# Attention and bilinear MoE on one core: seven products of halves in batch 1 too, and two units of w moved from stage 2 into stage 1

## The chip, the cores and the metric

The kernel runs on one core of a Trainium2 chip. The metric is the device time of one execution in microseconds (us), lower being better; the output must agree with the reference in shape, type and value.

A core has a matrix engine (TensorE, PE in the profile), a vector engine (VectorE, DVE), a scalar engine (ScalarE, ACT), GpSimd (POOL, unused here) and SyncE (SP), which in this kernel only issues transfers (DMAs). Matmuls write into PSUM, from which VectorE and ScalarE read.

## The reference

Eight batches of 512 tokens with 8 heads of 64, and 32 state rows for each batch and head. Attention in both directions gives 512 + 32 rows of 512 for each batch, and a bilinear expert turns each row into 512 outputs:

```python
scores = scale * x @ state.T;  a = softmax(scores);   xread = a @ state
scores2 = scale * state @ x.T; a2 = softmax(scores2); sread = a2 @ x
rows = concatenate([xread, sread], axis=2)          # heads merged: 4608 rows of 512
h = ((rows @ w1) * (rows @ w2)) @ w3                # 512 -> 1024 -> 1024
out = h @ w_out                                     # 1024 -> 512
```

The kernel folds w3 and w_out into one matrix of 1024 x 512 (`wo`), and the state of a batch with w1 and w2 into `sw`, so that (a @ state) @ w1 becomes a @ (state @ w1). All large products are made of three float32r matmuls (hi x lo, hi x hi, lo x hi), for which each operand is split: `split` is a ScalarE cast to `hi` (L97) and a VectorE subtract to `lo` (L98).

## The kernel before, in words

The program has a prologue (weights are converted, batch 0's attention and stage 1 run), then batches 0 to 7 in turn, then the 256 state rows (`state_rows`). A batch has these parts:

- **Stage 1** (`stage1_sums`, L301): eight tiles `ft` of 128 columns of the 1024; each takes 12 matmuls of 128x512 (L310) into a two-bank PSUM tile (`two_banks`, pool `ps_2`, three tiles in rotation). ScalarE copies one bank out (L394, or L291 in a plain batch), VectorE multiplies it with the other.
- **Stage 2, plain** (`stage2`, L328): four tiles `tt` of 128 tokens, 24 matmuls of 128x512 each (L324). Batches 0 and 1 have it.
- **Stage 2 by quarters** (`stage2_quarters`, L434): seven products of half-size operands (a Strassen-like scheme: a11, s3, a12, a22, s2, s1, s4), 24 matmuls of 128x256 each (`product`, L428). Batches 2 to 7 have it (`fast_batch`, L490). It needs sums and differences of halves of the hidden values, made in `hidden_quarters` (L389) and during stage 2, and of halves of `wo`, made once by `combine_weights(k)` for k = 0 to 3 (two sums L371, four differences L377, one split into `t_hi` and `t_lo`). Before, k = 0 and 1 are made in batch 1's stage 1, after ft 3 and ft 7, and k = 2 and 3 in its stage 2.
- **Attention of the next batch**, hidden among the above: `scores` (8 matmuls L147 on each half of the rows, then maxima and exponentials), its softmax sums (from L210), `at` (transpose L221 and split), a transpose and 16 block moves by SyncE (L228, L171), and `read_state` of the present batch (`reads[b]`, 64 small matmuls L243, L248, L252, 16 moves).
- **w of the next batch** (`sw_steps`, L264): four units w[0] to w[3]. A unit is a two-bank PSUM tile filled by 16 matmuls of 64x32 weights (L147), and a split of 128x1024 from it, whose cast and subtract both read PSUM. Stage 1's ft 0 to 3 use w[0] and w[1], ft 4 to 7 use w[2] and w[3].

In `fast_batch` reads[b] and scores stand after ft 3; `stage2_quarters` runs w[0], w[1] and the softmax after its first product (a11), and w[2] and w[3] after the second (s3).

TensorE and SyncE run in the order in which the code is written (`manual_schedule`). ScalarE's and VectorE's order is set by a scheduler when the program is built, with priority for the lines under `tc.high_priority()`; on the chip each engine runs its list in order, and waits where a semaphore tells it to. A PSUM tile is written again only when all readers of what it held are done. `x_d`, `x_s` and `e2` have one buffer each, `st` two; their loads are issued after ft 3 (`load_tokens`, `load_x`), those of batches 1 and 2 before that at the end of batch 0's stage 2.

Of the kernel before, what the change touches and what calls it, by code (L numbers as in the profile page):

```python
# [29 lines left out]
P = 128  # L30
# [3 lines left out]
LAST = 5  # L34
PARTS = {0: (640, 1024), 1: (512, 1024)}
WARM = 15
PLAIN = 2

@with_exitstack
def attn_bilinear_kernel(  # L40
# [302 lines left out]
    def side_steps(b):


        if b == B:
            return [[reads[b - 1]], [], [], []]
        scores, reads[b], a2 = attention_steps(b)
        w = sw_steps(b)
        softmax = scores()  # L350
        first = partial(islice, softmax, 3)
        if b == 1:
            def rest():

                with tc.issue_after(stored[0].ins):
                    yield from softmax

            return [[first], [reads[0], w[0], w[1]], [], [rest], [w[2], w[3]], []]

        product = partial(islice, softmax, 1)  # L360
        loads = [partial(load_tokens, b), partial(load_x, b + 1)]
        return [[w[0], w[1], product, reads[b - 1], *loads, w[2], w[3], lambda: softmax], [], [], []]
# [23 lines left out]
    def by_two(t):  # L386
        return t.rearrange("p (k n) -> p k n", k=2)

    def hidden_quarters(ps, ft, q):  # L389
        a_sb = tmp_tile()  # L390
        p, kk = divmod(ft, 2)
        first, second = slice(0, HT), slice(HT, S)
        with tc.high_priority():
            nc.scalar.copy(out=a_sb, in_=ps[:, 0])  # L394
            if ft < QF:
                if kk == 0:
                    q["raw"].append(main.tile([P, 2, NF], F32, name="g_x", bufs=2))
                nc.vector.tensor_tensor(out=q["raw"][p][:, kk], in0=a_sb, in1=ps[:, 1], op=ALU.mult)  # L398
            else:
                if ft == QF:  # L400
                    q["r22"] = late.tile([P, QF, HT], F32, name="r22")
                nc.vector.tensor_tensor(out=a_sb[:, first], in0=a_sb[:, first], in1=ps[:, 1, first], op=ALU.mult)  # L402
                nc.vector.tensor_tensor(out=q["r22"][:, ft - QF], in0=a_sb[:, second], in1=ps[:, 1, second], op=ALU.mult)
        if ft == 0:
            q["a11"], q["s3"] = quarter_pairs(), quarter_pairs()
        elif ft == QF:
            q["a12"] = quarter_pairs()
        if ft >= QF:
            split(*(t[:, kk] for t in q["a12"][p - 2]), a_sb[:, first])
            if kk:  # L410
                i = p - 2
                raw, r22 = q["raw"][i], q["r22"][:, 2 * i:2 * i + 2]
                nc.vector.tensor_tensor(out=raw[:, :, second], in0=raw[:, :, second], in1=r22, op=ALU.add)
                nc.vector.tensor_tensor(out=raw[:, :, first], in0=raw[:, :, second], in1=raw[:, :, first], op=ALU.subtract)
        elif kk:
# [3 lines left out]
            nc.vector.tensor_tensor(out=s3, in0=raw[:, :, first], in1=raw[:, :, second], op=ALU.subtract)
            split(*q["s3"][p], s3)  # L420
# [11 lines left out]
                    )  # L432

    def stage2_quarters(b, q, units):  # L434
        half = lambda o: slice(o * HO, (o + 1) * HO)
        b_part = lambda i, o: (lambda part, k: wo[part][:, i * QF + k, half(o)])
        t_part = lambda j: (lambda part, k: t_parts[part][:, j, k])
        sum2 = lambda out, x, y: nc.vector.tensor_tensor(out=out, in0=x, in1=y, op=ALU.add)  # L438
        c11, c21, m7, m1 = (tmp_tile() for _ in range(4))

        def stored_quarter(o, rows, cols):
            for tt in range(2):
                first = (2 * rows + tt) * P
# [12 lines left out]
        run(units[3:])
# [58 lines left out]
    def batch_stage2(b, gs):  # L515
        side = side_steps(b + 1)
        for tt in range(NT):
            stage2(gs, tt, [(out[b, tt * P:(tt + 1) * P], 0, P)])
            run(side[tt])
            if tt in (1, 2):  # L520
                combine_weights(tt + 1)


    with tc.tile_pool(name="pro", bufs=2) as pro:
# [108 lines left out]
        for tt in range(NT):
            dests = [(out[0, tt * P:(tt + 1) * P], 0, P)]
            if tt in early:
                store(acc[tt], dests)
            else:
                stage2(gs, tt, dests)
            run(side[tt])
        load_tokens(1)  # L640
        load_x(2)
    late = ctx.enter_context(tc.tile_pool(name="late", bufs=1))
    t_parts = {part: late.tile([P, 4, QF, HO], F32R, name=f"t_{part}") for part in ("hi", "lo")}


    def state_rows():
        n = B * NS
# [4 lines left out]
        for ft in range(FT):  # L652
            quarter, c = divmod(ft * P, NQ)
            ps = two_banks()
            for i in range(2):
# [7 lines left out]
            gs.append([g[:, :n] for g in new_g(ft)])  # L663
# [4 lines left out]
            nc.vector.tensor_tensor(out=sums[:, 0], in0=sums[:, 0], in1=sums[:, 1], op=ALU.mult)  # L668
            split(*gs[-1], sums[:, 0])
# [59 lines left out]
```

## Time and profile before

| | |
|---|---|
| time, median of 3 runs | 496.94 us (496.57 to 497.07) |
| the profiled execution | 496.68 us, span 494.9 us, granted TensorE clock 0.999 |
| batches 1, 2 (first stage 1 matmul to the next batch's) | 49.44, 49.43 us |
| batches 3 to 6 | 48.80 us each |

The span runs from the first to the last instruction in the profile. "PE busy" counts matmuls; "PEld" is the loading of weights, which overlaps. In the timeline a row is: start, busy time, engine, line, operation, out<-in, shapes, count; what stands in brackets is the idle time ahead of the row and what ended it. Matmuls are pipelined, so a row's busy time is longer than the distance to the next row's start, and the distances are what counts.

### The profile page before, as it was taken

The page shows a single profiled execution, that of the slowest core. Times are in us where ns is not written, and L with a number is a line of the kernel's source. Part 1 is how long each engine was busy: PE and PEld are TensorE (multiplying, and loading weights), DVE is VectorE, ACT ScalarE, POOL GpSimd, SP SyncE. Part 2 cuts the span into 40 slices and gives each one's busy share as a digit, 9 for nine tenths or more (in the row PEclk, how much of TensorE's full clock was granted, in tenths as well). Part 3 has the DMA queues.
Part 4 walks back from the last instruction along what each step waited for, and adds up shares of the span by engine and source line. Part 5 has one row for each costly group of instructions (what it writes and reads, how often), then busy time and mean ns, then how long its engine had stood idle before and what let it go on. Part 6 is the DMA issues. An engine that isn't in the chain of part 4 may idle for free.

```text
span 494.9 us, 8790 instructions
## 1 busy us (share of the span) xinstructions
PE 486.4 (98%) x3486; PEld 376.0 (76%) x3486; DVE 375.3 (76%) x584; ACT 238.8 (48%) x371; POOL 0.2 (0%) x4
## 2 busy tenths in 40 slices
PE   8999999999999999999999999999999999999996
PEld 5444467777876868897789778977897888899885
DVE  5669896772679889956995799479948994687770
ACT  4767784443544346613651365137513751453650
POOL 0000000000000000000000000000000000000000
PEclk9999999999999999999999999999999999999999
DMA  8996971013500721430233033303330222001101
GB/s 340 363 386 228 366 280 31 13 47 77 187 8 19 235 50 41 160 110 3 88 114 108 2 110 99 101 3 107 112 90 2 91 52 78 4 3 46 42 1 42
DMA packets 55785, 52.48 MB, mean 106 GB/s; under 512 B 42688, under 2 KB 49856, under 8 KB 51136
## 3 DMA queue, kind: packets, MB, share of 16 engines
q1 hardware_dynamic: 47488, 43.27, 26.6%
q10 hardware_dynamic: 8256, 8.65, 5.0%
q8 instruction: 27, 0.44, 0.4%
q14 instruction: 14, 0.11, 0.1%
HBM read 38.27 MB, written 8.91 MB: 95 GB/s over the span
## 4 chain that ended last, share of the span: by engine, by line
PE 83%; DVE 9%; DMA 3%; ACT 2%; issue 1%; SPq 1%; ACTq 0%; DVEq 0%
PE ps L310 29%; PE ps_o L428 20%; PE ps_o L324 8%; PE ps L147 6%; PE ps_o L555 6%; PE ps L661 3%; PE ps L428 3%; PE ps_o L542 3%; PE ps L542 3%; DMA e<-work 2%; PE ps L662 2%; DVE work L187 1%; DVE m L204 1%; DVE m L190 1%; SPq L171 1%
## 5 line engine op out<-in xcount | busy, mean ns | idle before, releaser
L310 PE MATMUL ps<-at_lo,sw_hi 128*128 128x512 f32 x256 | 101.2, 395 | 0.8 <-ACT g_hi L97 0.8
L310 PE MATMUL ps<-at_hi,sw_hi 128*128 128x512 f32 x256 | 99.7, 390 | 0.0
L310 PE MATMUL ps<-at_hi,sw_lo 128*128 128x512 f32 x256 | 99.6, 389 | 0.0
L394 ACT COPY tmp<-ps 128x512 f32<-128x512 f32 x48 | 28.1, 588 | 89.1 <-PE ps L310 54.4
L310 PEld LDWEIGHTS ps<-at_lo,sw_hi 128*128 128x128 f32 x256 | 48.1, 188 | 17.3 <-DVE g_x L398 3.4
L310 PEld LDWEIGHTS ps<-at_hi,sw_lo 128*128 128x128 f32 x256 | 48.1, 188 | 10.1
L310 PEld LDWEIGHTS ps<-at_hi,sw_hi 128*128 128x128 f32 x256 | 48.1, 188 | 9.6 <-issue 0.2
L97 ACT CAST g_hi<-g_x 128x512 fp32r<-128x512 f32 x48 | 29.2, 621 | 39.5 <-DVE g_x L467 20.4
L398 DVE TENSOR_TENSOR g_x<-tmp,ps 128x512 f32<-128x512 f32 x24 | 16.4, 687 | 36.2 <-ACT tmp L394 36.2
L97 ACT CAST g_hi<-tmp 128x256 fp32r<-128x256 f32 (+1 forms) x54 | 27.1, 503 | 32.4 <-DVE tmp L402 16.8
L98 DVE TENSOR_TENSOR sw_lo<-ps,sw_hi 128x1024 fp32r<-128x1024 f32 (+1 forms) x34 | 38.3, 1149 | 5.2 <-ACT sw_hi L97 5.2
L98 DVE TENSOR_TENSOR g_lo<-g_x,g_hi 128x512 fp32r<-128x512 f32 x48 | 31.6, 682 | 3.1 <-ACT g_hi L97 2.8
L98 DVE TENSOR_TENSOR g_lo<-tmp,g_hi 128x256 fp32r<-128x256 f32 (+1 forms) x54 | 28.8, 535 | 6.2 <-ACT g_hi L97 5.6
L97 ACT CAST sw_hi<-ps 128x1024 fp32r<-128x1024 f32 (+1 forms) x34 | 31.3, 967 | 4.2 <-PE ps L147 4.1
L147 PE MATMUL ps<-w_sb,st 64*32 64x512 f32 (+1 forms) x544 | 31.4, 570 | 0.0
L428 PE MATMUL ps_o<-wo_lo,g_hi 128*128 128x256 f32 x144 | 29.6, 287 | 0.5 <-DVE tmp L438 0.5
L428 PE MATMUL ps_o<-t_lo,g_hi 128*128 128x256 f32 x144 | 29.5, 287 | 0.0
L428 PE MATMUL ps_o<-t_hi,g_hi 128*128 128x256 f32 x144 | 29.0, 283 | 0.0
L428 PE MATMUL ps_o<-wo_hi,g_hi 128*128 128x256 f32 x144 | 29.0, 283 | 0.0
L428 PE MATMUL ps_o<-wo_hi,g_lo 128*128 128x256 f32 x144 | 29.0, 283 | 0.0
L428 PE MATMUL ps_o<-t_hi,g_lo 128*128 128x256 f32 x144 | 29.0, 283 | 0.0
L555 PE MATMUL ps_o<-w_sb,w 128*128 128x512 f32 x64 | 28.5, 599 | 0.0
(113 smaller groups left out, 912.6 us busy)
## 6 DMA issues: line engine op xcount, KB each, us to landing
raw<-in_w_k_dram SPq DMA_DIRECT2D x8, 1024.0 KB, 6.8
x_d<-in_x_d_dram SPq DMA_DIRECT2D x8, 1024.0 KB, 7.0
raw<-in_w_dram SPq DMA_DIRECT2D x8, 1024.0 KB, 6.4
x_s<-in_x_s_dram SPq DMA_DIRECT2D x8, 1024.0 KB, 5.3
out_dram<-tmp ACTq DMA_DIRECT2D x48, 128.0 KB, 2.0
raw<-in_w3t_dram SPq DMA_DIRECT2D x4, 1024.0 KB, 7.5
e<-work SPq DMA_DIRECT2D x96, 32.0 KB, 2.0
sread<-turned SPq DMA_DIRECT2D x128, 4.0 KB, 1.7
```

The source lines that it names most:

```text
L97: nc.scalar.copy(out=hi, in_=src),
L98: nc.vector.tensor_tensor(out=lo, in0=src, in1=hi.bitcast(F32), op=ALU.subtract),
L147: nc.tensor.matmul(ps[j * NS:(j + 1) * NS, q], sts[b][rows, j], moving(rows, j), start=True, stop=True)
L310: nc.tensor.matmul(ps[:, i], w[:, kt, c:c + P], a[:, kt], start=(k == 0), stop=(k == 3 * KT - 1))
L324: nc.tensor.matmul(ps[:, :DO], g, wo[w][:, ft, :], start=(ft == 0 and k == 0), stop=(ft == FT - 1 and k == 2))
L394: nc.scalar.copy(out=a_sb, in_=ps[:, 0])
L398: nc.vector.tensor_tensor(out=q["raw"][p][:, kk], in0=a_sb, in1=ps[:, 1], op=ALU.mult)
L428: nc.tensor.matmul(ps[:, tt * HO:(tt + 1) * HO], g[:, tt * P:(tt + 1) * P], w(part, k), start=(fresh and k == 0 and n == 0 and tt == 0), s ...
L542: nc.tensor.matmul(w34_ps[i][:, :DO], chunks[k][:, DO + i * P:DO + (i + 1) * P], w_out[k], start=(k == 0), stop=(k == FT - 1),)
L555: nc.tensor.matmul(w34_ps[i][:, :DO], w3s[i][:, k * P:(k + 1) * P], w_out[k], start=(k == 0), stop=(k == FT - 1))
L661: nc.tensor.matmul(ps[:, i], wh[:, ks], sr[:, kt], start=(kt == 0), stop=False)
L662: nc.tensor.matmul(ps[:, i, :n], wl[:, ks], sr[:, kt, 1], start=False, stop=(kt == NP - 1))
```

## The change

- `PLAIN` falls from 2 to 1: batch 1 has its stage 2 by quarters too. `batch_stage2` is gone, `fast_batch` is now `quarter_batch`.
- The sums of halves of `wo` are made earlier: k = 0, 1, 2 after tt 0, 1, 2 of batch 0's plain stage 2, k = 3 after ft 1 of batch 1. The pool `late` is opened before batch 0's stage 2.
- In each quarter batch w[0], reads[b] and w[1] stand after ft 3, ahead of scores; w[2], w[3] and the softmax stand after the a11 product, and nothing after s3.
- One step of the softmax (its exponentials' end) is asked for after ft 4, the next ones only in stage 2.
- In the state rows the output tiles are allocated later; `a2["t"]` of batch 1 is an `e2` tile.

```diff
-PLAIN = 2
+PLAIN = 1
...
-    def fast_batch(b):
+    def quarter_batch(b):
         q = {"raw": []}
+        w = sw_steps(b + 1) if b + 1 < B else [lambda: None] * 4
         softmax = iter(())
         for ft in range(FT):
-            hidden_quarters(stage1_sums(b, ft), ft, q)
+            ps = stage1_sums(b, ft)
+            a_sb = tmp_tile()
+            with tc.high_priority():
+                nc.scalar.copy(out=a_sb, in_=ps[:, 0])
+            hidden_quarters(a_sb, ps[:, 1], ft, q)
             if ft == QF - 1:
-                reads[b]()
+                run([w[0], reads[b], w[1]])
                 if b + 1 < B:
                     scores, reads[b + 1], _ = attention_steps(b + 1)
                     softmax = scores()
...
-            elif ft in (QF, QF + 2):
+            elif ft == QF:
                 next(softmax, None)
-
-        units = sw_steps(b + 1) if b + 1 < B else []
-        stage2_quarters(b, q, units[:2] + [lambda: softmax] + units[2:])
+            if b == PLAIN and ft == 1:
+                combine_weights(QF - 1)
+        stage2_quarters(b, q, [*w[2:], lambda: softmax])
...
         product(bank_a, q["a11"], b_part(0, 0), True)
         nc.scalar.copy(out=m1, in_=bank_a)
-        run(units[:3])
+        run(units)
...
-        run(units[3:])
         product(bank_a, q["a12"], b_part(1, 0), False)
...
-        load_tokens(1)
-        load_x(2)
     late = ctx.enter_context(tc.tile_pool(name="late", bufs=1))
     t_parts = {part: late.tile([P, 4, QF, HO], F32R, name=f"t_{part}") for part in ("hi", "lo")}
 
+    for tt in range(NT):
...
+            stage2(gs, tt, dests)
+        run(side[tt])
+        if tt + 1 < QF:
+            combine_weights(tt)
+    load_tokens(1)
+    load_x(2)
...
-    for b in range(1, PLAIN):
-        gs = []
-        for ft in range(FT):
-            stage1(b, ft, gs)
-            if ft % 4 == 3:
-                combine_weights(ft // 4)
-        batch_stage2(b, gs)
     for b in range(PLAIN, B):
-        fast_batch(b)
+        quarter_batch(b)
```

How the built programs differ at three places follows. Line numbers after the change are smaller: L394 is L489 there, L398 is L389, L402 and L403 are L393 and L394, L419 is L410, L371 and L377 are L363 and L369.

TensorE in batch 3 between ft 3 and ft 4 (`ps_2033`, `ps_2123` before and `ps_2163`, `ps_2279` now are the tiles of ft 3 and ft 4), before:

```order
L310 MATMUL ps_2033<-at_hi,sw_hi 128x512
L310 MATMUL ps_2033<-at_hi,sw_lo 128x512
L243 MATMUL ps_o<-x_s,e_1727 32x64 x32
L147 MATMUL ps_2108<-x_d,st 32x512 x8
L310 MATMUL ps_2123<-at_lo,sw_hi 128x512
L310 MATMUL ps_2123<-at_hi,sw_hi 128x512
```

and now:

```order
L310 MATMUL ps_2163<-at_hi,sw_lo 128x512
L147 MATMUL ps_2185<-w_sb,st 32x512 x8
L243 MATMUL ps_o<-x_s,e_1883 32x64 x32
L147 MATMUL ps_2251<-w_sb,st 32x512 x8
L147 MATMUL ps_2264<-x_d,st 32x512 x8
L310 MATMUL ps_2279<-at_lo,sw_hi 128x512
```

Two units of w, each in a two-bank tile of its own, have come in around the read. (The listing counts pairs of small matmuls once.)

VectorE in batch 3 from ft 3's multiply to those of ft 4, before (`ps_2108` is scores' tile):

```order
L398 TENSOR_TENSOR g_x<-tmp,ps_2033 128x512
L419 TENSOR_TENSOR tmp<-g_x 128x512
L248 TENSOR_TENSOR scaled<-ps_o,sum_1588 128x128
L98 TENSOR_TENSOR g_lo<-g_x,g_hi 128x512
L98 TENSOR_TENSOR g_lo<-tmp,g_hi 128x512
L252 STREAM_TRANSPOSE turned<-scaled 128x128
L187 STREAM_TRANSPOSE work<-ps_2108 128x1024
L190 TENSOR_REDUCE m_2149<-ps_2108 128x2
L204 TENSOR_REDUCE m_2156<-work 128x32
L402 TENSOR_TENSOR tmp<-tmp,ps_2123 128x256
L403 TENSOR_TENSOR r_2138<-tmp,ps_2123 128x256
```

and now (`ps_2185` and `ps_2251` are the tiles of w[0] and w[1], `ps_2264` scores'):

```order
L410 TENSOR_TENSOR tmp<-g_x 128x512
L98 TENSOR_TENSOR g_lo<-g_x,g_hi 128x512
L98 TENSOR_TENSOR sw_lo<-ps_2185,sw_hi 128x1024
L98 TENSOR_TENSOR g_lo<-tmp,g_hi 128x512
L248 TENSOR_TENSOR scaled<-ps_o,sum_1744 128x128
L252 STREAM_TRANSPOSE turned<-scaled 128x128
L98 TENSOR_TENSOR sw_lo<-ps_2251,sw_hi 128x1024
L187 STREAM_TRANSPOSE work<-ps_2264 128x1024
L190 TENSOR_REDUCE m_2305<-ps_2264 128x2
L204 TENSOR_REDUCE m_2312<-work 128x32
L393 TENSOR_TENSOR tmp<-tmp,ps_2279 128x256
L394 TENSOR_TENSOR r_2294<-tmp,ps_2279 128x256
```

Two subtracts of 128x1024 have come in between ft 3's multiply and ft 4's. ScalarE's list at the same place is now the a11 cast, w[0]'s cast, s3's cast, w[1]'s cast and ft 4's copy:

```order
L97 CAST g_hi<-g_x 128x512
L97 CAST sw_hi<-ps_2185 128x1024
L97 CAST g_hi<-tmp 128x512
L97 CAST sw_hi<-ps_2251 128x1024
L489 COPY tmp<-ps_2279 128x512
```

where the two casts of w were absent before.

VectorE in batch 1 ahead of w[0]'s subtract, now (`r_1009` and `t_lo` are the sums of halves for k = 3, `ps_1016` and `ps_1033` the tiles of ft 2 and ft 3, `ps_1055` w[0]'s):

```order
L389 TENSOR_TENSOR g_x<-tmp,ps_1016 128x512
L369 TENSOR_TENSOR r_1009<-tmp 128x256 x2
L369 TENSOR_TENSOR r_1009<-tmp,r_1009 128x256
L389 TENSOR_TENSOR g_x<-tmp,ps_1033 128x512
L369 TENSOR_TENSOR r_1009<-tmp,r_1009 128x256
L410 TENSOR_TENSOR tmp<-g_x 128x512
L98 TENSOR_TENSOR g_lo<-g_x,g_hi 128x512
L98 TENSOR_TENSOR t_lo<-r_1009,t_hi 128x4x256
L98 TENSOR_TENSOR g_lo<-tmp,g_hi 128x512
L98 TENSOR_TENSOR sw_lo<-ps_1055,sw_hi 128x1024
```

and before, at the same ft 2 and ft 3 (`ps_965` and `ps_985`), with plain hidden values (L292) and k = 0:

```order
L292 TENSOR_TENSOR tmp<-tmp,ps_965 128x512
L98 TENSOR_TENSOR g_lo<-tmp,g_hi 128x512
L371 TENSOR_TENSOR tmp<-wo_hi,wo_lo 128x512
L292 TENSOR_TENSOR tmp<-tmp,ps_985 128x512
L371 TENSOR_TENSOR tmp<-wo_hi,wo_lo 128x512
L377 TENSOR_TENSOR r_1009<-tmp 128x256
```

There the sums of k = 0 followed ft 3's multiply, and no unit of w stood in stage 1.

More of the change, by code (lines that the diff above doesn't have):

```diff
@@ L341, in attn_bilinear_kernel, with side_steps, rest @@
     reads = {}
[L343 to L349, printed above, removed]
-        softmax = scores()
[L351 to L362, printed above, removed]
+    def side_steps():
+        scores, reads[1], _ = attention_steps(1)
+        w = sw_steps(1)
+        softmax = scores()
+        def rest():
+            with tc.issue_after(stored[0].ins):
+                yield from softmax
+        return [[partial(islice, softmax, 3)], [reads[0], w[0], w[1]], [], [rest], [w[2], w[3]], []]
     QF = FT // 2
@@ L387, in by_two, with hidden_quarters @@
         return t.rearrange("p (k n) -> p k n", k=2)
-    def hidden_quarters(ps, ft, q):
-        a_sb = tmp_tile()
+    def hidden_quarters(a, b, ft, q):
         p, kk = divmod(ft, 2)
@@ L393, in hidden_quarters @@
         with tc.high_priority():
-            nc.scalar.copy(out=a_sb, in_=ps[:, 0])
             if ft < QF:
@@ L397, in hidden_quarters @@
                     q["raw"].append(main.tile([P, 2, NF], F32, name="g_x", bufs=2))
-                nc.vector.tensor_tensor(out=q["raw"][p][:, kk], in0=a_sb, in1=ps[:, 1], op=ALU.mult)
+                nc.vector.tensor_tensor(out=q["raw"][p][:, kk], in0=a, in1=b, op=ALU.mult)
             else:
@@ L401, in hidden_quarters @@
                     q["r22"] = late.tile([P, QF, HT], F32, name="r22")
-                nc.vector.tensor_tensor(out=a_sb[:, first], in0=a_sb[:, first], in1=ps[:, 1, first], op=ALU.mult)
-                nc.vector.tensor_tensor(out=q["r22"][:, ft - QF], in0=a_sb[:, second], in1=ps[:, 1, second], op=ALU.mult)
+                nc.vector.tensor_tensor(out=a[:, first], in0=a[:, first], in1=b[:, first], op=ALU.mult)
+                nc.vector.tensor_tensor(out=q["r22"][:, ft - QF], in0=a[:, second], in1=b[:, second], op=ALU.mult)
         if ft == 0:
@@ L408, in hidden_quarters @@
         if ft >= QF:
-            split(*(t[:, kk] for t in q["a12"][p - 2]), a_sb[:, first])
+            split(*(t[:, kk] for t in q["a12"][p - 2]), a[:, first])
             if kk:
@@ L434, in stage2_quarters @@
     def stage2_quarters(b, q, units):
+        first, second = slice(0, HT), slice(HT, S)
         half = lambda o: slice(o * HO, (o + 1) * HO)
@@ L442, in stored_quarter @@
             for tt in range(2):
-                first = (2 * rows + tt) * P
-                nc.scalar.dma_start(out=out[b, first:first + P, half(cols)], in_=o[:, half(tt)])
+                start = (2 * rows + tt) * P
+                nc.scalar.dma_start(out=out[b, start:start + P, half(cols)], in_=o[:, half(tt)])
         bank_a = bank()
@@ L460, in stage2_quarters @@
         s2 = quarter_pairs()
-        s = [raw[:, :, 0:HT] for raw in q["raw"]]
+        s = [raw[:, :, first] for raw in q["raw"]]
         for i in range(2):
@@ L470, in stage2_quarters @@
         for i in range(2):
-            split(*s1[i], q["raw"][i][:, :, HT:S])
+            split(*s1[i], q["raw"][i][:, :, second])
         bank_d = two_banks()[:, 0]
@@ L513, in run @@
                 pass
[L515 to L521, printed above, removed]
     with tc.tile_pool(name="pro", bufs=2) as pro:
@@ L621, in attn_bilinear_kernel @@
             if quarter == 1:
-                side = side_steps(1)
+                side = side_steps()
             elif quarter == 2:
@@ L632, in attn_bilinear_kernel @@
         early_stage2(QT - 1)
[L633 to L639, printed above, removed]
-        load_tokens(1)
-        load_x(2)
     late = ctx.enter_context(tc.tile_pool(name="late", bufs=1))
     t_parts = {part: late.tile([P, 4, QF, HO], F32R, name=f"t_{part}") for part in ("hi", "lo")}
+    for tt in range(NT):
+        dests = [(out[0, tt * P:(tt + 1) * P], 0, P)]
+        if tt in early:
+            store(acc[tt], dests)
+        else:
+            stage2(gs, tt, dests)
[4 more added lines that the diff above has]
+    load_x(2)
     def state_rows():
@@ L662, in state_rows @@
                     nc.tensor.matmul(ps[:, i, :n], wl[:, ks], sr[:, kt, 1], start=False, stop=(kt == NP - 1))
-            gs.append([g[:, :n] for g in new_g(ft)])
             sums = main.tile([P, 2, n], F32, name="tmp", bufs=4)
@@ L668, in state_rows @@
             nc.vector.tensor_tensor(out=sums[:, 0], in0=sums[:, 0], in1=sums[:, 1], op=ALU.mult)
+            gs.append([g[:, :n] for g in new_g(ft)])
             split(*gs[-1], sums[:, 0])
```

## The prediction

> **What bounds the kernel now.** I read the busy shares and the chain of waits first, then the windows of whole batches, and the timeline of one batch last.
>
> ```profile
> span 494.9 us, 8790 instructions
> PE 486.4 (98%) x3486; PEld 376.0 (76%) x3486; DVE 375.3 (76%) x584; ACT 238.8 (48%) x371; POOL 0.2 (0%) x4
> PE 83%; DVE 9%; DMA 3%; ACT 2%; issue 1%; SPq 1%; ACTq 0%; DVEq 0%
> ```
>
> TensorE is busy 98% of the span and holds 83% of the chain, so a change counts by the TensorE time it removes and by the waits it puts there. VectorE, at 76%, is the one that could make it wait. The windows run from one batch's first stage 1 matmul to the next's: batches 1, 2 and 3, then 6, which equals 4 and 5 in length. The last row is batch 3's second half of stage 1. The columns are the stretch, its length, busy time of PE, PEld, DVE, ACT and POOL, granted clock, DMA share, GB/s.
>
> ```profile
> 119.31:168.75 49.44, 49.44 (x337) 38.06 (x336) 37.84 (x58) 21.70 (x33) 0.00 (x0) 1.00 0.29 90
> 168.75:218.18 49.43, 48.58 (x409) 40.43 (x408) 42.97 (x68) 23.64 (x40) 0.00 (x0) 1.00 0.39 114
> 218.18:266.98 48.80, 48.60 (x410) 40.23 (x409) 39.55 (x63) 21.90 (x37) 0.00 (x0) 1.00 0.25 76
> 364.58:413.38 48.80, 48.60 (x410) 40.23 (x409) 39.55 (x63) 21.89 (x37) 0.00 (x0) 1.00 0.21 56
> 231.23:242.70 11.47, 11.27 (x57) 9.04 (x49) 11.44 (x23) 5.76 (x13) 0.00 (x0) 1.00 0.04 6
> ```
>
> Batches already in quarters cost 48.80 us, batch 1 costs 49.44: a quarter batch is only 0.64 us cheaper, and VectorE is busy 11.44 of 11.47 us in its second half of stage 1. That is just where the change puts two more units of w. The clock is 1.00 everywhere.
>
> **Batch 1's products.**
>
> ```profile
> 119.31 0.39 PE L310 MATMUL ps<-at_lo,sw_hi 128*128 128x512 f32 x1
> 141.07 0.39 PE L324 MATMUL ps_o<-wo_lo,g_hi 128*128 128x512 f32 x1
> ```
>
> Between these rows lie the 96 matmuls of stage 1: 21.76 us, 0.2267 each; stage 2's 96 of the same shape cost 21.76 too. The quarters are 7 x 24 = 168 of 256 columns. Their price stands in batch 3, whose TensorE pieces I need anyway:
>
> ```profile
> 229.18 1.10 PE L243 MATMUL ps_o<-x_s,e 128*32 128x64 f32 x64
> 230.21 1.09 PE L147 MATMUL ps<-x_d,st 64*32 64x512 f32 x16
> 231.23 0.50 PE L310 MATMUL ps<-at_lo,sw_hi 128*128 128x512 f32 x1
> ...
> 237.17 0.47 PE L310 MATMUL ps<-at_lo,sw_hi 128*128 128x512 f32 x1 [0.20 <-ACT g_hi L97]
> ...
> 242.70 0.40 PE L428 MATMUL ps_o<-wo_lo,g_hi 128*128 128x256 f32 x2
> ...
> 245.66 1.95 PE L147 MATMUL ps<-w_sb,st 64*32 64x512 f32 x32
> 247.54 0.51 PE L428 MATMUL ps_o<-t_lo,g_hi 128*128 128x256 f32 x2
> ...
> 250.60 1.95 PE L147 MATMUL ps<-w_sb,st 64*32 64x512 f32 x32
> 252.48 0.51 PE L428 MATMUL ps_o<-wo_lo,g_hi 128*128 128x256 f32 x2
> ```
>
> Read 1.03, scores 1.02, a burst of two w units 1.88. From 252.48 to 266.98 five products take 14.50: 2.98 for the one behind a burst, 2.88 for the others, so 0.120 a matmul. Stage 2 by quarters costs 168 x 0.120 = 20.16 against 21.76, **1.60 us** less in batch 1. The Trainium skill ("Perfetto Trace Analysis", section "Optimizing Tensor Performance", Matmuls) speaks against this part: larger matmuls are more efficient than smaller ones. The trace agrees, since 0.120 is more than half of 0.2267: at equal efficiency the gain would be 2.7 us, and by the rule alone batch 1 would lose. By the rows the lower count still wins 1.6.
>
> **Fewer bursts.** A burst costs a change into it and one out of it: 0.10 in the product behind it (2.98 against 2.88) and 0.08 to 0.10 ahead (a11 from 242.70 takes 2.96). Stage 2 of a batch falls from 266.98 - 242.70 = 24.28 to 2.96 + 1.88 + 2.98 + 5 x 2.88 = **22.20**. Stage 1 gets two units more: w0 1.02, read 1.03, then w1 and scores together 1.88, so 3.93 where 2.05 stood. By TensorE alone a batch gains 24.28 - 22.20 - 1.88 = 0.20.
>
> **The waits behind w0 and w1, batches 3 to 6.** Three two-bank PSUM tiles rotate. Now scores, ft 4 and ft 5 each take a tile from a stage 1 multiply long done. In the changed program ft 4 takes w0's tile and waits for w0's sw_lo subtract, ft 5 waits for w1's; ft 6, as now, waits for the second multiply of ft 4. Call M the time after ft 3 when w0 starts, 229.18 in batch 3.
>
> ```profile
> 229.96 0.69 DVE L398 TENSOR_TENSOR g_x<-tmp,ps 128x512 f32<-128x512 f32 x1 [2.09 <-ACT tmp L394]
> 230.69 0.69 DVE L419 TENSOR_TENSOR tmp<-g_x 128x512 f32<-128x512 f32 x1
> 231.29 0.28 DVE L248 TENSOR_TENSOR scaled<-ps_o,sum 128x128 f32<-128x128 f32 x1
> 231.50 0.68 DVE L98 TENSOR_TENSOR g_lo<-g_x,g_hi 128x512 fp32r<-128x512 f32 x1
> ...
> 232.70 0.30 DVE L252 STREAM_TRANSPOSE turned<-scaled 128x128 f32<-128x128 f32 x1
> 232.93 1.21 DVE L187 STREAM_TRANSPOSE work<-ps 128x1024 f32<-128x1024 f32 x1
> 234.06 1.18 DVE L190 TENSOR_REDUCE m<-ps 128x2 f32<-128x1024 f32 x1
> 235.17 1.20 DVE L204 TENSOR_REDUCE m<-work 128x32 f32<-128x1024 f32 x1
> 236.28 0.40 DVE L402 TENSOR_TENSOR tmp<-tmp,ps 128x256 f32<-128x256 f32 x1
> 236.61 0.41 DVE L403 TENSOR_TENSOR r<-tmp,ps 128x256 f32<-128x256 f32 x1
> ```
>
> Steps from start to start: 0.60 for 512 elements, 0.21 and 0.23 for L248 and L252, 1.13 for 1024, 1.11 for a reduce, 0.33 for 256. L403 ends at 237.02, ft 6 starts 0.15 later at 237.17: that is today's wait. It costs 11.47 - 11.0 = 0.47 in the window above, against 10.88 for 48 matmuls and 0.1 for the change of shape.
>
> ```profile
> 230.69 0.62 ACT L97 CAST g_hi<-g_x 128x512 fp32r<-128x512 f32 x1 [0.76 <-DVE g_x L398]
> ...
> 247.74 1.92 ACT L97 CAST sw_hi<-ps 128x1024 fp32r<-128x1024 f32 x2
> ...
> 249.93 2.34 DVE L98 TENSOR_TENSOR sw_lo<-ps,sw_hi 128x1024 fp32r<-128x1024 f32 x2
> ```
>
> Two casts in 1.92 are a step of 0.91 and one of 1.01; two subtracts in 2.34 are 1.13 and 1.21. In the changed program ScalarE's cast of w0 stands behind the a11 cast, which starts at M + 1.51 and hands on 0.52 later (0.62 less the 0.10 by which rows overlap, as in the two casts). So sw_hi(w0) runs from M + 2.03 to M + 3.05, sw_lo(w0) from M + 3.07 to M + 4.28, and ft 4 starts at **M + 4.43**, 0.50 behind the M + 3.93 at which TensorE is through. Queued behind that matmul are all others; VectorE goes on meanwhile. Its order then is s3_lo 0.60, L248 0.21, L252 0.23, sw_lo(w1) 1.13, L187 1.13, two reduces 2.22, the two multiplies of ft 4 (0.33 and 0.41). From M + 4.20 these sum to M + 10.46, so ft 6 starts at **M + 10.61**, where TensorE alone would be there at M + 4.43 + 0.10 + 5.44 = M + 9.97. Two more tiles follow as in batch 3 (242.70 - 237.17 = 5.53): stage 2 starts at M + 16.14, now M + 13.52, so +2.62. The sum of a batch: 2.62 - (24.28 - 22.20) = **+0.54**, four times, +2.16. In stage 2 VectorE loses two subtracts, so nothing there gets later.
>
> **Batch 2.**
>
> ```profile
> 180.88 1.05 PE L243 MATMUL ps_o<-x_s,e 128*32 128x64 f32 x58 [0.85 <-DMA e<-work]
> ```
>
> Its read waits 0.85 us for moved blocks, which come late out of batch 1's plain stage 2. With quarters they leave at the place where batch 2 sends off batch 3's, and batch 3's read (229.18) shows no wait. I take the steady length, 11.00 + 16.14 + 22.20 = 49.34: **-0.09**.
>
> **Batch 1's stage 1.** The loads for batch 2 are issued late:
>
> ```profile
> 126.22 0.43 SPq L153 DMA_DIRECT2D st<-in_st_dram  x1
> ...
> DMA to landing us min/median/max: 5.0/5.0/5.0
> ```
>
> st lands at 131.2, and w0 would start at M = 119.31 + 10.88 + 0.09 = 130.28: about 1 us of wait. SyncE issues ahead of it, before and after the change, 32 block moves, the second 16 of them from here on:
>
> ```profile
> 114.87 10.67 SPq L171 DMA_DIRECT2D work<-work  x16
> ```
>
> Their source is a transpose behind batch 1's at_lo; at_lo ends at 109.33 (row below), the transpose 1.1 later, so it may slip by 4 us before st slips. combine_weights(3) now runs between ft 1 and ft 3. The last of it, a t_lo like the next row, stands ahead of sw_lo(w0):
>
> ```profile
> 136.14 1.23 DVE L98 TENSOR_TENSOR t_lo<-r,t_hi 128x1024 fp32r<-128x1024 f32 x1 [0.26 <-ACT t_hi L97]
> ```
>
> VectorE from ft 3's multiply at 131.06 (M + 0.78): 0.60, L369 0.33, L410 0.60, a11_lo 0.60, with 0.19 for the wait on t_hi t_lo starts at 133.38, 1.13, s3_lo 0.60, sw_lo(w0) 135.12 to 136.33, ft 4 at 136.48. Without waits ft 4 would start at 134.21, so 2.27 us are lost, st's wait within them. ft 6 then is not held again: VectorE's chain ends at 141.9, TensorE is there at 142.0. Stage 2 starts at 147.5, batch 2 at 169.7, now 168.75: **+1.0**; without the wait it would be -1.3.
>
> **combine_weights in batch 0's stage 2.** Three sets, each two of 0.60, four of 0.33, a 1.13 subtract on VectorE (3.65) and a 0.95 cast on ScalarE, lie in VectorE's idle time:
>
> ```profile
> 108.10 1.23 DVE L98 TENSOR_TENSOR at_lo<-work,at_hi 128x1024 fp32r<-128x1024 f32 x1 [1.67 <-ACT at_hi L97]
> ...
> 114.10 2.35 DVE L98 TENSOR_TENSOR sw_lo<-ps,sw_hi 128x1024 fp32r<-128x1024 f32 x2 [3.63 <-ACT sw_hi L97]
> 122.85 0.69 DVE L292 TENSOR_TENSOR tmp<-tmp,ps 128x512 f32<-128x512 f32 x1 [6.40 <-ACT tmp L291]
> ```
>
> 11.70 us idle for some 11 us of work. at_lo ends near 109.7, needed at 119.31; the sw_lo end near 119, their tiles are needed from 124. I cost it at **0**; without that cover the spill, at most 1 us, would show before batch 1's ft 2.
>
> **Sum.** Batch 1 +1.0, batch 2 -0.09, batches 3 to 6 +2.16, batch 7 and what follows unchanged: **+3.1 to 3.2**. The profiled execution took 496.68 (span 494.9 and 1.8 around it), 0.26 below the median of the runs, 496.94. So 496.7 + 3.2 = **499.9 us**.
>
> **Rivals.** *Faster (B):* ScalarE and VectorE hand w0's tile back by M + 3.93. The point is a sw_lo(w0) start at M + 2.57, not 3.07, with ft 4's multiplies through by M + 9.35. Then batch 1 gives -1.3, batch 2 -0.8, the four -0.2 each: 493.8, and 491.9 if today's ft 6 wait goes too. For it: ScalarE idles 0.76 before the a11 cast. Against it: its order has that cast first. *Only w0's wait stays (C):* VectorE has ft 4's multiplies done by M + 9.82, 0.64 ahead of my chain, and ft 6 is not held: 0.64 less in five batches, 496.7; for it speaks only that the sum has eleven terms. *It half cancels (E):* batch 1 comes out even and the steady batches lose half: 499.9 - 1.0 - 1.1 = 497.8. *Batch 1's loads land later (D):* the transpose slips past 114.87, and ft 4 of batch 1 waits 2 to 3 us more: 502 to 503; against it stand the 4 us of slack. That the change doesn't do what it says is excluded: the order of the instructions shows the moved units and the seven products.
>
> **How the numbers follow.** Forecast, 498.6 to 501.2: 0.62 (each of five batches may be off by 0.25); B 0.13, C 0.10, D 0.08, E 0.07. The likeliest is 499.9. The range 496.5 to 502.0 takes in C and E and leaves out B and most of D, 0.2 together. A measurement of this kernel tells about 0.2%, 1 us, from no change: 495.9 to 497.9 is the same. C and E lie there, so same 0.15 (their edges give a little away), faster 0.13, slower 0.72.
>
> **What would show it.** Right: ft 4's first matmul in batches 2 to 6 with some 0.4 us idle behind sw_lo, ft 6's with 0.6 behind a VectorE chain, steady batches of 49.3, batch 1 of 50.4 with its longest wait ahead of ft 4, batch 2's read without a DMA wait. Wrong: steady batches under 48.8, or ft 4 without a wait.

## The result, and the profile after

| | time, us (median) | ratio to the kernel before, 95% interval |
|---|---|---|
| before | 496.93 (496.57 to 497.07, 6 runs) | |
| changed | 500.34 (500.15 to 501.73, 6 runs) | 1.0074 [1.0061, 1.0087] |

The change makes the kernel slower by 3.4 us, 0.7%. The profiled execution took 500.2 us (span 498.4), against 496.68 (494.9) before: +3.5.

The page of the changed kernel, the same lines as before (busy shares, then the chain by engine):

```profile
PE 485.2 (97%) x3558; PEld 377.7 (76%) x3558; DVE 388.1 (78%) x611; ACT 240.0 (48%) x378; POOL 0.2 (0%) x4
...
PE 76%; DVE 11%; ACT 5%; DMA 5%; issue 1%; SPq 0%; DVEq 0%; ACTq 0%
```

TensorE is busy 1.2 us less and the span is 3.5 longer: the TensorE time was saved as planned, and waits took its place. The view of waits, TensorE's own (who it waited for, sum in us, times, longest), names them:

```profile
PE ps L310 <- ACT g_hi L97: 3.2, 5, 0.7
PE ps L310 <- DVE sw_lo L98: 2.9, 6, 1.2
...
PE ps L147 <- DMA st<-in_st_dram: 0.8, 1, 0.8
```

Before, the first of these was 0.8 in four waits and the other two did not exist. The five waits put down to `g_hi` are those of ft 6. Each stands 0.15 us behind VectorE's second multiply of ft 4, as below, while the `g_hi` cast is a reader of another buffer.

The windows by batch (stretch, length, busy PE, PEld, DVE, ACT, POOL, clock, DMA share, GB/s), batches 1, 2, 3 and 6:

```profile
119.88:170.35 50.47, 48.48 (x409) 40.20 (x408) 45.20 (x75) 24.21 (x40) 0.00 (x0) 1.00 0.39 121
170.35:219.83 49.48, 48.48 (x410) 40.18 (x409) 39.68 (x63) 21.52 (x37) 0.00 (x0) 1.00 0.26 80
219.83:269.31 49.48, 48.48 (x410) 40.18 (x409) 39.68 (x63) 21.53 (x37) 0.00 (x0) 1.00 0.26 78
...
368.31:417.83 49.52, 48.52 (x411) 40.19 (x410) 39.70 (x63) 21.53 (x37) 0.00 (x0) 1.00 0.20 57
```

TensorE is busy 0.1 us less in a steady batch than before (48.48 against 48.60), and idle 1.0 us where it was idle 0.2. TensorE's timeline of batch 3, from w[0] (M = 230.83) over ft 4 to ft 6:

```profile
230.83 1.09 PE L147 MATMUL ps<-w_sb,st 64*32 64x512 f32 x16
...
235.18 0.50 PE L310 MATMUL ps<-at_lo,sw_hi 128*128 128x512 f32 x1 [0.35 <-DVE sw_lo L98]
...
241.57 0.47 PE L310 MATMUL ps<-at_lo,sw_hi 128*128 128x512 f32 x1 [0.65 <-ACT g_hi L97]
```

VectorE's at the same place:

```profile
233.90 1.23 DVE L98 TENSOR_TENSOR sw_lo<-ps,sw_hi 128x1024 fp32r<-128x1024 f32 x1 [0.22 <-ACT sw_hi L97]
235.04 0.68 DVE L98 TENSOR_TENSOR g_lo<-tmp,g_hi 128x512 fp32r<-128x512 f32 x1
...
236.19 1.19 DVE L98 TENSOR_TENSOR sw_lo<-ps,sw_hi 128x1024 fp32r<-128x1024 f32 x1
237.31 1.23 DVE L187 STREAM_TRANSPOSE work<-ps 128x1024 f32<-128x1024 f32 x1
238.46 1.19 DVE L190 TENSOR_REDUCE m<-ps 128x2 f32<-128x1024 f32 x1
239.57 1.20 DVE L204 TENSOR_REDUCE m<-work 128x32 f32<-128x1024 f32 x1
240.69 0.41 DVE L393 TENSOR_TENSOR tmp<-tmp,ps 128x256 f32<-128x256 f32 x1
241.01 0.41 DVE L394 TENSOR_TENSOR r<-tmp,ps 128x256 f32<-128x256 f32 x1
```

w[0]'s subtract starts at M + 3.07 and ends at 235.13; ft 4 follows 0.05 later. VectorE then runs without a gap worth naming to 241.42, and ft 6 starts 0.15 behind it.

### The profile page after: what moved, and what is told of

It reads as the page before. It is cut to its first block, busy times and chain, and to the rows that moved or that the text cites. A ratio compares the mean times of both kernels' runs of the same rounds, so it can differ in the third digit from the quotient of the medians.

```text
span 498.4 us, 8999 instructions
## 1 busy us (share of the span) xinstructions
PE 485.2 (97%) x3558; PEld 377.7 (76%) x3558; DVE 388.1 (78%) x611; ACT 240.0 (48%) x378; POOL 0.2 (0%) x4
## 4 chain that ended last, share of the span: by engine, by line
PE 76%; DVE 11%; ACT 5%; DMA 5%; issue 1%; SPq 0%; DVEq 0%; ACTq 0%
PE ps L310 29%; PE ps_o L419 24%; PE ps_o L324 7%; PE ps L419 4%; PE ps L147 4%; DMA raw<-in_w_k_dram 3%; PE ps L651 3%; PE ps_o L543 3%; DVE sw_lo L98 2%; DMA raw<-in_w3t_dram 2%; PE ps L652 2%; DVE work L187 1%; DVE m L204 1%; DVE m L190 1%; ACT ulps L126 1%
## 5 line engine op out<-in xcount | busy, mean ns | idle before, releaser
L489 ACT COPY tmp<-ps 128x512 f32<-128x512 f32 x56 | 32.9, 588 | 115.8 <-PE ps L310 52.6
L389 DVE TENSOR_TENSOR g_x<-tmp,ps 128x512 f32<-128x512 f32 x28 | 19.3, 688 | 42.3 <-ACT tmp L489 42.3
L97 ACT CAST g_hi<-g_x 128x512 fp32r<-128x512 f32 x56 | 33.2, 622 | 25.8 <-DVE g_x L389 10.6
L98 DVE TENSOR_TENSOR g_lo<-g_x,g_hi 128x512 fp32r<-128x512 f32 x56 | 36.5, 689 | 1.6 <-ACT g_hi L97 1.4
L419 PE MATMUL ps_o<-t_lo,g_hi 128*128 128x256 f32 x168 | 34.5, 287 | 0.0
L419 PE MATMUL ps_o<-wo_hi,g_hi 128*128 128x256 f32 x168 | 33.9, 283 | 0.0
L419 PE MATMUL ps_o<-t_hi,g_lo 128*128 128x256 f32 x168 | 33.9, 283 | 0.0
L419 PE MATMUL ps_o<-t_hi,g_hi 128*128 128x256 f32 x168 | 33.8, 283 | 0.0
L419 PE MATMUL ps_o<-wo_hi,g_lo 128*128 128x256 f32 x168 | 33.8, 283 | 0.0
L419 PE MATMUL ps_o<-wo_lo,g_hi 128*128 128x256 f32 x168 | 33.8, 283 | 0.0
L419 PEld LDWEIGHTS ps_o<-t_lo,g_hi 128*128 128x128 f32 x168 | 26.1, 192 | 5.0 <-issue 5.0
```

The costliest lines, as they stand in the source:

```text
L97: nc.scalar.copy(out=hi, in_=src),
L98: nc.vector.tensor_tensor(out=lo, in0=src, in1=hi.bitcast(F32), op=ALU.subtract),
L389: nc.vector.tensor_tensor(out=q["raw"][p][:, kk], in0=a, in1=b, op=ALU.mult)
L419: nc.tensor.matmul(ps[:, tt * HO:(tt + 1) * HO], g[:, tt * P:(tt + 1) * P], w(part, k), start=(fresh and k == 0 and n == 0 and tt == 0), s ...
```

## The experiments

Theory: two more 128x1024 subtracts between ft 3 and ft 7 lengthen VectorE's list there, and TensorE waits for it, at ft 4 for w[0]'s tile and, what counts, at ft 6 for ft 4's multiplies. Rivals stand with each run. Lengths of batches are first stage 1 matmul to the next batch's, in the windows. Ratios are to the kernel before, run on the same chip.

| run | us | ratio, 95% interval | batch 1 | batch 3 |
|---|---|---|---|---|
| before (first profile) | 496.93 | | 49.44 | 48.80 |
| changed | 500.34 | 1.0074 [1.0061, 1.0087] | 50.47 | 49.48 |
| e1 w back in stage 2 | 498.30 | 1.0044 [1.0028, 1.0060] | 52.10 | 48.80 |
| e2 only w moved | 499.76 | 1.0064 [1.0049, 1.0079] | 49.42 | 49.49 |
| e3 w[0]'s cast first | 498.78 | 1.0047 [1.0031, 1.0064] | 50.47 | 49.26 |
| e4 scores after ft 1 | 506.41 | 1.0200 [1.0185, 1.0215] | 50.47 | 50.80 |
| g1 reduce behind ft 4 | 496.72 | 0.9993 [0.9984, 1.0003] | 50.27 | 48.84 |
| g2 k = 3 in batch 0 | 500.43 | 1.0065 [1.0048, 1.0082] | 50.13 | 49.52 |
| g3 w back, k = 3, loads | 496.46 | 0.9985 [0.9975, 0.9994] | 50.22 | 48.80 |
| g4 g3 and reduce behind | 494.05 | 0.9937 [0.9917, 0.9958] | 50.41 | 48.34 |
| h1 g4, loads still earlier | 492.54 | 0.9905 [0.9890, 0.9920] | 48.75 | 48.35 |
| h2 w kept in stage 1 | 494.49 | 0.9949 [0.9934, 0.9964] | 49.25 | 48.61 |
| h3 changed, loads earlier | 501.77 | 1.0087 [1.0062, 1.0111] | 51.85 | 49.51 |
| j1 before, reduce, loads | 496.00 | 0.9978 [0.9968, 0.9989] | 49.44 | 48.34 |

**e1 and e2, the two halves of the change apart.**

```diff
# e1, on the changed kernel
-        run(units)
+        run(units[:3])
...
+        run(units[3:])
         product(bank_a, q["a12"], b_part(1, 0), False)
...
-                run([w[0], reads[b], w[1]])
+                reads[b]()
...
-        stage2_quarters(b, q, [*w[2:], lambda: softmax])
+        stage2_quarters(b, q, [w[0], w[1], lambda: softmax, w[2], w[3]])
# e2, on the kernel before
-                reads[b]()
+                run([w[0], reads[b], w[1]])
...
-            elif ft in (QF, QF + 2):
+            elif ft == QF:
...
-        stage2_quarters(b, q, units[:2] + [lambda: softmax] + units[2:])
+        stage2_quarters(b, q, [*w[2:], lambda: softmax])
```

> The changed kernel with w[0] and w[1] put back behind the a11 product, and w[2], w[3] behind s3; batch 1 stays in quarters, the sums of halves stay early. Theory (two units of w in stage 1 make TensorE wait for VectorE): batches 3 to 6 return to 48.8 us each, batch 2 to 48.8 as well, ft 4 has no wait behind sw_lo and ft 6 waits 0.4 again. Batch 1 then shows the wait for its loads instead, since scores needs x_d at once: some 50.8 us. In all about 497.5 us, 2.8 below the changed kernel and 0.1% above the one before. Rival (the seven products in batch 1 and the early sums of halves are what costs): the steady batches stay at 49.5 and the time at 500.

> The kernel before, batch 1 plain, with only the new place of w: w[0], read, w[1], scores after ft 3, w[2], w[3] and softmax behind a11. Theory: +0.70 us in each of batches 3 to 6; batch 2 has the same new wait but w[0] ahead of the read hides the 0.85 us wait for moved blocks, so it comes out at 49.5, where it was 49.43. In all +2.9 us, 499.8. Rival (the new place costs nothing by itself, the loss comes from batch 1): 496.9.

e2 gave 499.76 for 499.8, and its batches 2 to 6 are 49.47 to 49.52: the new place of w, with the softmax step that goes with it, makes the loss without any change in batch 1. e1's steady batches returned to 48.80 to 48.83, except batch 4 with 49.09, so the rival fell. But batch 1 took 52.10 where I had 50.8, and the whole 498.30 for 497.5. The waits there are 1.6 us for x_s and 0.9 for x_d: batch 1 in quarters needs its loads at once.

**e3 and g1, which of the two waits counts.** e3 puts w[0]'s cast ahead of the a11 cast; g1 puts one reduce of scores behind ft 4's multiplies.

```diff
# e3
+            if ft == QF - 1 and PLAIN < b < B - 1:
+                run([w[0]])
+                w[0] = lambda: None
+                with tc.issue_after(sw_casts[b + 1, 0, 0].ins):
+                    split(*q["a11"][p], raw[:, :, first])
...
# g1
+            with tc.issue_after(gate[-1].ins) if gate else ExitStack():
                 nc.vector.tensor_reduce(out=m1, in_=s1v, axis=AX.X, op=ALU.max)
...
-                nc.vector.tensor_tensor(out=q["r22"][:, ft - QF], in0=a[:, second], in1=b[:, second], op=ALU.mult)
+                gate.append(nc.vector.tensor_tensor(out=q["r22"][:, ft - QF], in0=a[:, second], in1=b[:, second], op=ALU.mult))
```

> The changed kernel with the cast of w[0] ahead of ft 3's a11 cast on ScalarE, and so w[0]'s subtract ahead of a11's on VectorE, in batches 2 to 6. Theory (VectorE's chain up to ft 4's multiplies sets the end of stage 1, ft 4's wait lies inside it): the 0.35 us wait at ft 4 goes, ft 6 comes only 0.25 earlier, at M + 10.5, since VectorE saves no more than its idle 0.2 to 0.3; 49.25 us a batch, in all -1.2, 499.1. Rival (each wait counts by itself): 0.42 less in each of five batches, 49.07 us, in all -2.1, 498.2.

> The changed kernel with one VectorE instruction moved: scores' second reduce (1.11 us) stands behind the two multiplies of ft 4 instead of ahead of them. Nothing else moves, w[0] and w[1] stay in stage 1. Theory (the wait at ft 6 is VectorE's chain up to those multiplies): the chain ends 1.1 us earlier, at M + 9.5, ft 6 no longer waits, ft 4's 0.35 stays: 0.8 us less in each of batches 2 to 6, 48.7 a batch, in all 496.3. Rival (the three PSUM tiles with two units of w among them are what holds TensorE, and the wait only moves to ft 5 or ft 7): 499.5 to 500.3.

In e3 the wait at ft 4 is gone, and ft 6 waits longer instead, as its row in batch 3 shows:

```profile
240.57 0.47 PE L311 MATMUL ps<-at_lo,sw_hi 128*128 128x512 f32 x1 [0.77 <-ACT g_hi L97]
```

A batch gained 0.22 us (49.26 for 49.48), the idle that VectorE lost ahead of sw_lo, and not the 0.42 of ft 4's wait. In g1 the wait at ft 6 is gone: batch 3's second half of stage 1 takes 11.04 us, with VectorE still busy in nearly all of it:

```profile
234.80:245.84 11.04, 11.04 (x49) 9.09 (x49) 10.94 (x22) 5.08 (x12) 0.00 (x0) 1.00 0.04 6
```

Its time, 496.72 where 496.3 was expected, takes back the changed kernel's whole loss (ratio 0.9993 to the kernel before) by the order of one VectorE instruction. So the last step of a list sets the end, and a wait ahead of it is inside it.

**e4, a better spread that is worse.**

```diff
             if ft == QF - 1:
-                run([w[0], reads[b], w[1]])
+                run(w[:2])
+            if ft == (QF - 1 if b == PLAIN else 1):
+                reads[b]()
...
```

> The changed kernel with read and scores after ft 1 in batches 2 to 6, and w[0], w[1] after ft 3 in one burst. scores' transpose and two reduces (3.4 us of VectorE) then lie ahead of ft 3, where VectorE is idle for 2 us before each pair of tiles, and ft 4 takes a tile that no unit of w holds. Theory: the waits at ft 4 and ft 6 both go, one burst more in stage 1 costs 0.2: 48.4 to 48.6 us a batch in batches 3 to 6, in all about -4.5 to -5, 495.5. Rival (w's subtracts hold ft 6 wherever scores stands): ft 6 still waits 0.4 to 0.6, 49.2 us a batch, 499.

A miss by 11 us, worse than either forecast. TensorE now waits 0.47 us ahead of w[1] for scores' exponentials, and at ft 5, in stage 1's second half, for the tile of w[0], whose subtract comes later still:

```profile
241.12 0.50 PE L310 MATMUL ps<-at_lo,sw_hi 128*128 128x512 f32 x1 [1.18 <-DVE sw_lo L98]
```

VectorE ahead of that, in the same batch:

```profile
237.52 1.21 DVE L213 TENSOR_REDUCE sum<-work 128x32 f32<-128x1024 f32 x1
238.65 0.68 DVE L98 TENSOR_TENSOR g_lo<-g_x,g_hi 128x512 fp32r<-128x512 f32 x1
239.25 0.68 DVE L98 TENSOR_TENSOR g_lo<-tmp,g_hi 128x512 fp32r<-128x512 f32 x1
239.85 2.35 DVE L98 TENSOR_TENSOR sw_lo<-ps,sw_hi 128x1024 fp32r<-128x1024 f32 x2
```

With scores early, the scheduler also drew the softmax's sum (L213) ahead of w's subtracts, which start 5.7 us after w[0] (234.18) where it was 3.07. How much of the 1.3 us a batch is that sum was not tried apart.

**g2 and h3, batch 1's stage 1.**

```diff
# g2
-        if tt + 1 < QF:
-            combine_weights(tt)
+        combine_weights(tt)
...
-            if b == PLAIN and ft == 1:
-                combine_weights(QF - 1)
# h3
+            if b == 0:
+                load_tokens(1)
             turned = att.tile([P, KT, D], F32, name="turned", bufs=1)
...
             elif quarter == 2:
                 run(side.pop(0))
+                load_x(2)
...
-    load_tokens(1)
-    load_x(2)
```

> The changed kernel with the last set of sums of halves (k = 3) made in batch 0's stage 2 too, after tt 3. Theory (in batch 1 its four differences and t_lo stand ahead of w[0]'s subtract, and st's wait lies inside that): ft 4 of batch 1 starts 1.2 us earlier, its wait behind sw_lo is gone, the 0.8 us wait for st stays: batch 1 takes 49.0 instead of 50.5, in all 498.9. Rival (the late load of st sets it): -0.2, 500.1.

> The changed kernel with only the loads issued as in h1. Theory (in batch 1 the late st and the k = 3 sums ahead of w[0]'s subtract hide one another): the wait for st goes, the one behind sw_lo at ft 4 grows by as much, batch 1 stays at 50.3 to 50.5, in all 500.1. Rival (st alone is what batch 1 lost): batch 1 at 49.5, 499.3.

g2's theory failed: batch 1 gained 0.34 us, not 1.5. The wait at ft 4 went, but st landed later in that run, and TensorE waited 1.40 us for it ahead of w[0] where it was 0.82:

```profile
132.91 1.09 PE L147 MATMUL ps<-w_sb,st 64*32 64x512 f32 x16 [1.40 <-DMA st<-in_st_dram]
```

h3 shows the other side. Without the wait for st, w[0] starts at once, at 130.74, and ft 4 waits the longer behind sw_lo, to 136.81, within 0.1 us of the changed kernel's 136.91:

```profile
130.74 1.09 PE L147 MATMUL ps<-w_sb,st 64*32 64x512 f32 x16
...
136.81 0.50 PE L312 MATMUL ps<-at_lo,sw_hi 128*128 128x512 f32 x1 [2.07 <-DVE sw_lo L98]
```

So the two lay side by side, and taking one away leaves the other. e3, e4 and g1 bear it out: TensorE idled 1.45 to 1.65 us ahead of w[0] there, and ft 4 still started 17.03 us into batch 1, as in the changed kernel. h3 was even slower, 501.77, which is told below under the hardware.

**g3, g4, h1, h2 and j1, towards a better version.** g3 is e1 with g2's edit and both loads issued ahead of batch 1's block moves; g4 adds g1's edit; h1 is g4 with h3's places for the loads; h2 is the changed kernel with the edits of e3, g1, g2 and h3; j1 is the kernel before with g1's and h3's.

```diff
# g3, beside e1 and g2
         run(side.pop(0))
+        load_tokens(1)
+        load_x(2)
         early_stage2(QT - 1)
```

> The kernel with w[0] and w[1] back in stage 2 (as in e1), the k = 3 sums in batch 0's stage 2, and batch 1's and 2's loads issued ahead of batch 1's block moves instead of behind them. Theory: the waits of 1.6 and 0.9 us for x_s and x_d that batch 1 had go, batch 1 takes 48.8 to 48.9 like the others, in all 495.0. If batch 1's products were no gain by themselves: 496.9 or more.

> g3 with scores' second reduce behind ft 4's multiplies as in g1. Theory: the wait of 0.47 us at ft 6, which the kernel before has as well, goes from batches 1 to 6: 48.35 us a batch, in all 492.2. Rival (VectorE then falls behind in stage 2, where its slack is 0.4 us): 494 to 495.

> g4 with the loads for batches 1 and 2 issued still earlier: st and x_d of batch 2 after batch 1's scores, x_s of batch 1 ahead of batch 0's sread moves, so that batch 1's block moves leave at the time they had before. Theory: the read's wait of 1.8 us for moved blocks in batch 1 goes and nothing takes its place: batch 1 takes 48.4 us like the others, in all 492.0, 1% below the kernel before. Rival (another late transfer shows behind it): 493.5 to 494.

> The changed place of w kept (w[0], read, w[1], scores after ft 3), with all that the runs so far took away: w[0]'s cast first (e3), scores' second reduce behind ft 4's multiplies (g1), the k = 3 sums in batch 0 (g2), and the loads as in h1. Theory (the place itself saves 0.2 us of TensorE a batch, and lost by VectorE's and ScalarE's order): no wait at ft 4 and ft 6, 48.15 to 48.2 us a batch, in all 491.2, 0.5 to 1 below h1. Rival (two more subtracts between ft 3 and ft 7 are too much for VectorE in any order): waits of 0.3 to 0.5 stay, 48.6 a batch, 494.

> The kernel before (batch 1 plain, w in stage 2, sums of halves as before) with scores' second reduce behind ft 4's multiplies and the loads as in h1; against h1 it tells what batch 1's seven products are worth once nothing waits for VectorE or the loads. Theory: batch 1 stays at 49.44 and batch 2 at 49.4 (its read waits 0.85 us for moved blocks out of the plain stage 2), batches 3 to 6 take 48.35; in all 497.0 - 4 x 0.45 = 495.2, so the seven products are worth some 2.5 us of h1's 4.5. Rival (they are worth nothing, the gate and the loads bring all): 492.5 to 493. Beside that, batch 7: with batch 1 plain the second store of its first quarter took 1.9 and 1.5 us to issue on ScalarE, and 0.45 in each program with batch 1 in quarters; if that hangs on how many stores went ahead, it takes over 1 us here too, if it is chance, 0.45.

g3 and g4 came out 1.5 and 1.9 us above the forecast, for one reason: the loads, put ahead of 16 block moves on SyncE's queue, delayed these, and batch 1's read waited for them (1.5 and 1.8 us for `e<-work`). The steady batches are as expected, 48.80 and 48.34. h1 mends it, and only a wait of 0.18 us, ahead of batch 1's last product, is left:

```profile
119.71:168.46 48.75, 48.57 (x409) 40.32 (x408) 45.17 (x75) 23.87 (x40) 0.00 (x0) 1.00 0.31 86
168.46:216.82 48.36, 48.36 (x410) 40.32 (x409) 39.43 (x63) 21.74 (x37) 0.00 (x0) 1.00 0.26 79
216.82:265.17 48.35, 48.35 (x410) 40.31 (x409) 39.43 (x63) 21.65 (x37) 0.00 (x0) 1.00 0.27 80
```

At 492.54 us it is the fastest, 0.95% below the kernel before. Against j1 (496.00, where 495.2 was expected) batch 1's seven products with the early sums are worth 3.5 us by the medians and 2.8 by the profiled executions. Of the latter 0.69 lies in batch 1 itself. 1.88 lies in batch 2 (50.24 against 48.36), where j1's read waits 1.3 us for blocks that leave its plain batch 1 late; that wait is no part of the products' own price.

h2 fell short of its theory, and its rival gave the numbers (48.6 a batch, 494): the view of waits has none at ft 4 or ft 6 in the steady batches, yet these take 48.61, 0.45 more than the 48.15 of TensorE's pieces. 0.2 is lost in the second half of stage 1 and 0.26 in stage 2's last two products (6.02 against 5.76 us). The trace of batch 3 shows VectorE there:

```profile
262.50 1.52 DVE L441 TENSOR_TENSOR tmp<-tmp,ps_o 128x512 f32<-128x512 f32 x2
...
263.33 0.48 PE L430 MATMUL ps_o<-wo_lo,g_hi 128*128 128x256 f32 x2
```

The kernel takes two single PSUM banks (pool `ps_o`) in turn, and the last product's is the one that the first of these two sums reads. That sum ends near 263.18, and the product starts 0.15 behind it, the distance that ft 6 keeps from ft 4's multiplies. Ahead of it VectorE was busy in 16.40 of 16.43 us. So the new place of w costs even in the best order found, 0.26 a batch against h1, and in stage 2 it is again VectorE that comes late.

## Why the prediction was right

It forecast 499.9, slower; 500.34 was measured. By its steps:

- **Steady batches.** +0.54 forecast, +0.68 to 0.72 measured. The mechanism holds to 0.1 us: w[0]'s subtract at M + 3.07 as forecast, ft 4 at M + 4.35 (4.43), ft 6 at M + 10.74 (10.61), stage 2 at M + 16.26 (16.14) and 22.22 long (22.20). The mis-sized term is the sum of VectorE's steps, M + 10.46, measured 10.59: nearly all of it is the step from L248 to L252, taken as 0.21 us from a place where another instruction stands between them, and 0.32 here, where one follows the other (235.64 and 235.96 above). Four batches make that 0.5 us. Stage 2's terms add up to 22.22 and not to the 22.20 written, and the three terms of the sum to 3.07, which was rounded up to 3.2; neither matters beside it.
- **Batch 2.** -0.09 forecast, +0.05 measured, for the same term; its read no longer waits.
- **Batch 1.** +1.0 forecast, 50.47 - 49.44 = +1.03 measured; st landed 5.1 us after its issue, and ft 4 came 17.03 us after the start of the batch, 17.17 forecast. g2, h3 and the starts of ft 4 in e3, e4 and g1 bear out that the two waits overlap.
- **Batch 0's stage 2.** 0 forecast. In the profiles TensorE's batch 1 starts 0.57 later, but that lead was there at batch 0's read already, ahead of all that the change moves; the starts in the twelve runs lie between 119.28 and 120.47.
- **Batch 7 and what follows, "unchanged".** This failed, to the change's favour: up to the state rows it takes 43.19 us, before 43.96. In the kernel before, ScalarE's pair of stores of the first quarter took 2.27 us to issue. Two casts (448.51) waited behind it (the row names PE for the 2.34 us, but ScalarE was issuing until 448.47), VectorE's list behind these, and the last product behind VectorE. Its rows before:

```profile
446.20 2.27 ACTq L444 DMA_DIRECT2D out_dram<-tmp  x2
448.51 1.14 ACT L97 CAST g_hi<-g_x 128x512 fp32r<-128x512 f32 x2 [2.34 <-PE ps_o L428]
454.40 0.47 PE L428 MATMUL ps_o<-wo_lo,g_hi 128*128 128x256 f32 x2 [0.55 <-DVE tmp L438]
```

and in the changed kernel, where no product of batch 7 waits:

```profile
450.64 0.82 ACTq L436 DMA_DIRECT2D out_dram<-tmp  x2
```

The two other programs with a plain batch 1 show the long issue too (1.91 in e2, 1.67 in j1); all those with quarters there have 0.82. So it goes with the plain batch 1. That the reason is the number of stores ahead (4 in a plain batch, 8 in quarters) is a guess that no run tried apart, and why it should cost 1 us stays open.

- **Rivals.** The faster one asked for w[0]'s tile back by M + 3.93 and ft 4's multiplies through by M + 9.35. e3 met the first and gained 0.22 a batch; g1 brought the multiplies through by M + 9.67 and gained 0.64: the second condition was the one that mattered. g1 is also the case of the rival in which only w0's wait stays: it asked for the multiplies by M + 9.82 and gave 0.64 less in five batches, 496.7. The rule quoted from the Trainium skill ("Perfetto Trace Analysis", on larger matmuls) did not decide: with the waits gone, batch 1 in quarters is 0.69 shorter (h1 against j1).

Summed over the profile: batches 1 to 6 +3.88, the start +0.57, batch 7 -0.77, the state rows and the end -0.18, together +3.5. The batches came out 0.8 above the 3.07 of their terms and the start 0.57 later, and batch 7 with the end, which were put at nothing, gave 0.95 back. The mechanism was right; that the total met the forecast to 0.4 us is in part luck.

## What to carry to other kernels

When work is moved on an engine that is 98% busy, list what it leaves on the others in the stretch where it lands, in their order, up to the next instruction that the busy engine waits for; here that list foretold the start of stage 2 to 0.12 us. A wait ahead of the last one in such a list costs nothing while the last one stands (e3): look for the instruction that can be put behind the awaited one (one reduce was worth 0.46 us a batch in g4, 0.64 in g1). Where two waits lie side by side, an experiment that takes one away says nothing about the other.

## What the runs showed of the hardware

In one profile the clock fell after a short idle time. In h3's batch 1 TensorE had some 4 us of small matmuls (64x32 and 128x32 weights), then 2.1 us without any, and then 3.6 us at a granted clock of 0.57:

```profile
130.74:134.70 3.96, 3.96 (x113) 1.60 (x112) 3.85 (x8) 3.10 (x5) 0.00 (x0) 1.00 0.02 4
134.70:136.81 2.11, 0.04 (x7) 0.01 (x1) 2.11 (x4) 1.40 (x2) 0.00 (x0) 1.00 0.00 0
136.81:140.41 3.60, 3.60 (x9) 2.82 (x10) 3.60 (x5) 0.00 (x0) 0.00 (x0) 0.57 0.03 5
```

The matmuls there follow one another at 0.43 us instead of 0.227, and the second half of stage 1 took 12.60 us against 11.22 in the changed kernel. That is h3's 1.4 us. Three of its four runs show a mean clock of 0.996 to 0.997 and 501.8 to 502.7 us; the fourth, at 1.00, took 500.35, about what the theory said. One execution of the changed kernel (501.73 us) and one of e1 (500.90) had a mean clock of 0.995 too; where it fell in them is not on record. Waits of 1.2 us (changed), 1.6 (e1) and 1.8 (g4) left the clock at 1.00 in their profiles. The Trainium skill ("TensorE: Matmul & The Clock Gate", Part 1) speaks of idle windows of some 3.4 us that run freely; here the clock fell after 2.1 us, behind small matmuls, and whether these count as idle is not known.
